# Centroid products moved behind the transposes, rounding steps and sums of x spread over the turns

## The chip, the cores and the metric

The kernel runs on one core of one Trainium2 chip. The metric is device microseconds of that core, the median of three runs: 996.82 us before the change (993.31 to 1000.97). The engines are called as the profile calls them: PE (matmul; PEld its weight loads), DVE (vector), ACT (scalar), POOL (GpSimd) and SP (here it only issues DMAs).

## The reference

Two blocks follow each other. The first is attention with a routing mask over 4 batches, 8 heads, 768 rows and 64 columns; each head has 16 centroids:

```
q_assign = argmax over c of  q_n . c_n      (q_n, k_n, c_n have length 1)
k_assign = argmax over c of  k_n . c_n
mask     = q_assign[:, None] == k_assign[None, :]
scores   = where(mask, q k^T / 8, -1e9)
attn     = softmax(scores);  x = attn v
```

A row thus attends to the rows that chose the same centroid. The second block takes x as 3072 rows of 512 columns:

```
h = x @ w_in            (512 to 2048)
g = h / (1 + exp(-1.702 h))
out = g @ w_out         (2048 to 512)
```

## The kernel before, in words

The kernel has two stages. The order of the instructions of every engine is the order in which the program issues them (a manual schedule), and each engine works through its own queue in that order.

**Attention.** Two heads of a batch are a pair; there are 16 pairs, 0 to 15. The loop over t (L636) has 96 turns and two more to drain. A turn takes two units. A unit is one block of 128 keys against half (384) of the queries, for both heads of the pair; six units, three turns, are a group, and two groups, six turns, are a pair. In what follows "turn 0" to "turn 5" are the six turns of a pair. In a turn the program issues, in this order:

- the scores of both units (L451), then the mask products (`part`, L466), which add a large negative number to the scores of pairs of rows with different centroids. They read rows of codes (`rows_of`) that DMAs have put in place;
- the exponentials on ACT (L474), and for the previous group the check of its row sums (`check`, L535 and L537, ACT);
- on POOL, the running sum of the exponentials over the six units of a group (`add_up`, L484, five additions of 128 x 768);
- the preparation of the next pair, if any is due in this turn (below);
- the value products of the two units of the turn before (L495), and after a group's last one a copy out of PSUM (L501);
- steps of the rounding of the weights (`step`, next paragraph);
- in turns 1 and 4, `normalise` of the group that ended: two row sums by matmul (L508), then on DVE a 32-block transposition (L511), a reciprocal (L513), a transposition back (L516) and a product (L522).

**Preparation of the next pair.** A list `PREP` has seven entries, and `prep_at` says in which of the six turns each is issued. Entries 0 and 1 are for q, 2 and 3 for k: one DVE transposition each of 128 x 768 (L305). Behind entry 1 and entry 3 the next load of q or k is issued (L134), ahead of entry 2 the load of v (L144), all on SP. Entry 4, `prep_near`, is the product of both with the centroids: eight small matmuls on PE (L326), sixteen records in the trace. Entry 5, `prep_assign`, is a chain on DVE from L349 to L389: the largest of the 16 products in each row, a code for the place where it stands, and its transposition. Entry 6, `prep_spread`, sends the codes through DRAM: four DMAs out (L396), then sixteen DMAs back (L403), which wait for the four. The mask products of the next pair need what these bring.

**Rounding.** The weights come in 64-bit form in 32 pieces. Each piece takes five DVE steps (L189, L193, L196, L200, L203), and `steps` says how many are issued in each of a pair's six turns. A piece begins with the issue of a later piece's load (L170), and its last step is followed by two instructions of ACT (L227, L230).

**PSUM and buffers.** `bank()` gives one of three PSUM banks in turn. Row sums, centroid products, assignment and rounding all take theirs there, so that the order of the calls says which bank a product has to wait for.

**Second block.** From L804 on, for each batch: matmuls of x with sums of w_in and of G with sums of w_out in seven products each (L716, L773), with the sums around them on DVE. For this the sums of x of a batch (`sums_x`, L598, with `differences`, L559) must stand: eight DVE instructions (L554). For the first batch they are issued in turn 76 of the attention; for the other batches between products of the batch before. The sums of the first weights (`sums_w`, L581) are four POOL instructions in each of the turns 72 and 78.

The functions that the change touches, and the loops that call them:

Of the kernel before, what the change touches and what calls it, by code (L numbers as in the profile page):

```python
# [38 lines left out]
def fast(  # L39
# [26 lines left out]
    nc = tc.nc  # L66
# [46 lines left out]
    def bank():  # L113
        return ps_m.tile([P, 512], FP32, name="m")

    def short():
        return tmp.tile([P, HALF], FP32, name="short")
# [154 lines left out]
    nc.vector.tensor_tensor(out=csq, in0=cent, in1=cent, op=ALU.mult)  # L272
    nc.vector.tensor_reduce(out=css, in_=csq, axis=AX.X, op=ALU.add)
    nc.gpsimd.tensor_tensor(out=cnorm, in0=css, in1=half, op=ALU.pow)
# [13 lines left out]
    for a in range(2):  # L288
# [4 lines left out]
                                         c=NC)[:, :, a, :])  # L293
# [3 lines left out]

    T, code, sT, hots = {}, {}, {}, {}

    def prep_turn(p, i):  # L300
        w, h = divmod(i, 2)
        if h == 0:
            T[p, w] = pairs.tile([P, S], FP32, name=f"T{w}")
            if p > 0:
# [41 lines left out]
    def prep_assign(p):  # L346
# [10 lines left out]
        best = asg.tile([P, n], FP32, name="best", bufs=1)  # L357
        nc.vector.tensor_reduce(out=best, in_=sc, axis=AX.X, op=ALU.max)
        eq = short().bitcast(BF16)[:, 0:n * NC].rearrange("p (n c) -> p n c",
# [8 lines left out]
        if p == 0:  # L368
            code[p] = asg.tile([P, n], FP32, name="code", bufs=1)
            nc.vector.tensor_reduce(out=code[p], in_=eq, axis=AX.X,  # L370
                                    op=ALU.max)
# [8 lines left out]
            in_=eq.rearrange("p (w j a) c -> p w j a c", a=2, j=NJ),  # L380
            axis=AX.X, op=ALU.max)
        nc.vector.scalar_tensor_tensor(
# [49 lines left out]
    PREP = [lambda p, i=i: prep_turn(p, i) for i in range(4)]  # L432
# [7 lines left out]
    s_of, A_of, sum_of, o_of, O_of, xT_of = {}, {}, {}, {}, {}, {}  # L440

    def split(g):
        return divmod(g, 2)
# [44 lines left out]
    def values(u):  # L488
        g, kt = divmod(u, NJ)
        p, h = split(g)  # L490
        if kt == 0:
            o_of[g] = ps_o.tile([P, 512], FP32, name="o")
        A = A_of.pop(u)
        for a in range(2):
            nc.tensor.matmul(out=o_of[g][a * D:(a + 1) * D, 0:HALF],  # L495
                             lhsT=v_in[p][:, a, kt, :], rhs=A[:, a, :],
                             start=(kt == 0), stop=(kt == NJ - 1))
        if kt == NJ - 1:
            O_of[g] = (xp if p < NPAIR - HP else xl).tile(
                [P, HALF], FP32, name="x")  # L500
            nc.scalar.copy(O_of[g], o_of.pop(g)[:, 0:HALF])  # L501

    def normalise(g):

        sm = sum_of.pop(g)
        ps = bank()
        for a in range(2):
            nc.tensor.matmul(out=ps[a * D:(a + 1) * D, 0:HALF], lhsT=twos,  # L508
                             rhs=sm[:, a, :], start=True, stop=True)
        turned = short()  # L510
        nc.vector.transpose(out=turned, in_=ps[:, 0:HALF])  # L511
        few = recs[g] = asg.tile([P, HALF // SQ], FP32, name="few")
        nc.vector.reciprocal(  # L513
            out=few, in_=turned.rearrange("p (n r) -> p n r", r=SQ)[:, :, 0])
        rec = short()
        nc.vector.transpose(  # L516
            out=rec.rearrange("p (n r) -> p n r", r=SQ),
            in_=few[:, :, None].broadcast_to((P, HALF // SQ, SQ)))
        p, h = split(g)
        b, hp = divmod(p, HP)  # L520
        x = O_of.pop(g)
        nc.vector.tensor_tensor(out=x, in0=x, in1=rec, op=ALU.mult)  # L522
        if b < B - 1:
            xT_of[b, h, hp] = x
        else:
            nc.sync.dma_start(out=kept[h, hp], in_=x)
# [25 lines left out]
    def sums(engine, todo):  # L552
        for o, a, op, b in todo:
            engine.tensor_tensor(out=o, in0=a, in1=b, op=(  # L554
                ALU.add if op == "+" else ALU.subtract))

    T_of = {}

    def differences(b):  # L559


        X = {(r, h, c): xT_of.pop((b, h, 2 * r + c))
             for r in range(2) for h in range(2) for c in range(2)}
        T = {(3, c): T_of[3, c] for c in range(2)}
        for c in range(2):
            T[1, c] = X[0, 1, c]
            sums(nc.vector, ((T[3, c], X[1, 1, c], "-", T[1, c]),
                             (T[1, c], T[1, c], "-", X[0, 0, c])))
        return X, T

    def A_in(row, col, f):

        at = (row * FB + f) * P
# [20 lines left out]

    def sums_x(b):  # L598

        X, T = differences(b)  # L600
        T.update(((i, c), T_of[i, c]) for i in (2, 4) for c in range(2))
        for c in range(2):
            sums(nc.vector, ((T[2, c], X[1, 1, c], "-", T[1, c]),))
        for c in range(2):
            sums(nc.vector, ((T[4, c], X[1, 0, c], "-", T[2, c]),))
        return X, T

    NT = NU // 2
    TG = NJ // 2

    prep_at = {}
    for p in range(1, NPAIR):
        for i in range(2 if p == 1 else 0, len(PREP)):
            t = 2 * TG * (p - 1) + (0, 0, 2, 2, 2, 3, 3)[i]
            prep_at.setdefault(t, []).append((p, i))
    loads = deque((p, w) for p in range(NPAIR) for w in range(2))
    for _ in range(3):  # L620
# [2 lines left out]
    def prep(p, i):  # L623
        if i == 2 and p:
            load_v(p)
        PREP[i](p)
        if i in (1, 3) and loads:
            load_qk(*loads.popleft())

    steps = (3, 1, 2, 0, 1, 4)  # L630
    XT = None
    for p, i in [(0, i) for i in range(6)] + [(1, i) for i in range(2)]:
        prep(p, i)
        if p == 0 and i in (1, 3):
# [1 line left out]
    for t in range(NT + 2):  # L636
        us = range(2 * t, 2 * t + 2) if t < NT else ()
        for u in us:
            scores(u)
        if t == 0:  # L640
            prep(0, 6)
        for u in us:
            part(u)
        for u in us:
            exps(u)
        if recs:
            check(*recs)
        for u in us:
            add_up(u)
        work = sorted(prep_at.get(t, ()), key=lambda w: PREP[w[1]] != prep_near)  # L650
        turns = [w for w in work if w[1] < 4]
        for p, i in turns:
            prep(p, i)
        work = [w for w in work if w[1] >= 4]
        while work and PREP[work[0][1]] == prep_near:
            prep(*work.pop(0))
        if 1 <= t <= NT:
            for u in range(2 * t - 2, 2 * t):
                values(u)
        if t in (NT - 24, NT - 18):  # L660
            sums_w(t // (NT - 18))
        if t == NT - 20:
            XT = sums_x(0)
        for p, i in work:
            prep(p, i)
        for _ in range(steps[t % (2 * TG)] if t > 2 else 0):
            step()
        if t >= 2 and (t - 2) % TG == TG - 1:
            normalise((t - 2) // TG)
# [134 lines left out]
    for b in range(B):  # L804
        for f in range(FB):
            first7(b, f, *XT)
            sums_w(b * FB + f + 2)
            if b == 0:
                sums_z(f)
        if b == 0:  # L810
            for h in range(2):
                for hp in range(HP):
                    x = xT_of[B - 1, h, hp] = xp.tile([P, HALF], FP32,
                                                      name="x")
                    nc.sync.dma_start(out=x, in_=kept[h, hp])
        for n in range(NH):
            sg = sums_g(n)
            if (b, n) == (B - 1, 0):


                ok = const.tile([P, 4, NW], FP32, name="ok")
                nc.vector.tensor_scalar(out=ok, in0=row_sums, scalar1=LIMIT,
                                        scalar2=None, op0=ALU.is_le)
                ok1 = const.tile([P, 1], FP32, name="ok1")
                nc.vector.tensor_reduce(out=ok1, in_=ok, axis=AX.XY, op=ALU.min)
            if (b, n) == (B - 1, 1):
                ps = bank()
                nc.tensor.transpose(out=ps[0:1, 0:P], in_=ok1, identity=ident)
                nc.vector.tensor_reduce(out=okt, in_=ps[0:1, 0:P], axis=AX.X,
                                        op=ALU.min)  # L830
                nc.vector.tensor_scalar(out=bad, in0=okt, scalar1=-1.0,
                                        scalar2=1.0, op0=ALU.mult, op1=ALU.add)
            if (b, n) == (B - 1, NH - 1):
                is_bad = nc.values_load(bad[0:1, 0:1], min_val=0, max_val=1)
            second7(b, n, sg)
            if n == 1 and b < B - 1:
                XT = sums_x(b + 1)
    return is_bad
@with_exitstack
def general(  # L840
# [436 lines left out]
```

## Time and profile before

| what | us |
|---|---|
| median of three runs | 996.82 |
| the profiled execution | 997.54 |
| its span, first to last instruction | 995.7 |
| start of pair 1's first turn | 38.90 |
| start of pair 15's first turn | 384.35 |
| first product of the second block | 409.30 |
| PE busy | 943.0 |
| DVE busy | 623.8 |
| POOL busy | 418.8 |
| ACT busy | 314.3 |

A line of a timeline is: start in us from the start of the span, time taken, engine, line of the kernel, operation, what is written and read, how many instructions are merged into the line, and in brackets the idle time before it and what ended it. A line of the waits is: who waited for whom, us in total, how often, the longest. In the slices of the span each digit is a fortieth of it, 24.9 us, in tenths of busy time; PEclk is the clock that PE was granted. Sums of busy time say little here, as PE is full in the second block and not in the first; so the turns are read one by one, from one first L451 to the next.

The turns of an ordinary pair are alike. In pair 9 they start at 231.95, 235.16, 239.01, 245.43, 248.63 and 252.48, and pair 10 starts at 255.69. Pairs 2 to 12 take 23.4 to 25.1 us each; pairs 13 and 14 take 31.7 and 25.6 us.

### The profile page before, as it was taken

Reading aid. Unit: us, or ns where it says so; the run is one execution under the profiler, and the core shown is the slowest. Engines: PE = TensorE matmul, PEld = TensorE weight load, DVE = VectorE, ACT = ScalarE, POOL = GpSimd, SP = SyncE. Lnnn points to the kernel's source line nnn. Section 1 sums busy time; section 2 is a strip of 40 time slices with the busy share of each in tenths; the row PEclk is TensorE's granted clock in tenths of the full one; section 3 lists DMA queues with packets and bytes.
Section 4 is the critical chain, followed back from the end, with each engine's and each line's share of the span. In section 5 each row is a group of like instructions: output and inputs, shape, how many; then the busy total and the mean of one; then the engine's idle time right before and its main releaser. Section 6 shows DMA issues by size and latency. Waiting matters only on the chain.

```text
span 995.7 us, 12731 instructions
## 1 busy us (share of the span) xinstructions
PE 943.0 (95%) x4565; PEld 569.6 (57%) x4565; DVE 623.8 (63%) x1029; ACT 314.3 (32%) x671; POOL 418.8 (42%) x308
## 2 busy tenths in 40 slices
PE   5998999999998789999999999999999999999997
PEld 3333333333333233455788655888655888556886
DVE  3678778877779985477634477534577434677431
ACT  3565565555655456322100122100222000222000
POOL 3878788777879678677400122000122000220000
PEclk8999999999999899999999999999999999999999
DMA  9344444544444311000200000000000000000000
GB/s 179 82 94 111 94 98 95 112 101 92 93 114 92 87 49 29 17 0 1 64 22 22 21 1 1 0 22 22 22 0 1 16 22 22 6 1 1 22 22 24
DMA packets 138440, 46.59 MB, mean 47 GB/s; under 512 B 127376, under 2 KB 132736, under 8 KB 138368
## 3 DMA queue, kind: packets, MB, share of 16 engines
q1 hardware_dynamic: 138224, 45.66, 20.2%
q8 instruction: 38, 0.62, 0.3%
q14 instruction: 34, 0.28, 0.1%
q10 hardware_dynamic: 144, 0.03, 0.0%
HBM read 37.63 MB, written 8.05 MB: 46 GB/s over the span
## 4 chain that ended last, share of the span: by engine, by line
PE 82%; DVE 12%; issue 3%; SPq 1%; DMA 1%; ACT 1%; POOL 0%; DVEq 0%; POOLq 0%; ACTq 0%
PE b L716 29%; PE b L773 29%; PE o L495 10%; PE s L451 9%; DVE T L305 2%; PE s L466 2%; PE m L508 2%; DVE short L516 1%; DVE short L511 1%; DVE e L200 1%; DVE x L522 1%; PE m L326 1%; DVE T L554 1%; DVE e L196 1%; DVE m L189 1%
## 5 line engine op out<-in xcount | busy, mean ns | idle before, releaser
L484 POOL TENSOR_TENSOR sum<-sum,A 128x768 f32<-128x768 f32 x128 | 243.3, 1901 | 32.0 <-ACT A L474 23.5
L474 ACT ACTIVATE A<-s 128x768 f32<-128x768 f32 x192 | 144.9, 806 | 158.6 <-PE s L466 157.0
L554 POOL TENSOR_TENSOR W<-w_in 128x256 f32<-128x256 f32 x32 | 23.8, 742 | 381.3 <-PE b L716 381.2
L707 DVE TENSOR_TENSOR G<-b,G 128x384 f32<-128x384 f32 x224 | 124.4, 556 | 64.6 <-PE b L716 51.4
L451 PE MATMUL s<-T,T 64*128 64x384 f32 x768 | 153.1, 518 | 4.4 <-ACT A L474 4.4
L495 PE MATMUL o<-A,inv 128*64 128x384 f32 x768 | 150.4, 515 | 0.0
L707 DVE TENSOR_TENSOR y<-b,y 128x256 f32<-128x256 f32 x72 | 29.4, 423 | 171.1 <-PE b L773 121.9
L544 ACT ACTIVATE th<-G 128x384 f32<-128x384 f32 x128 | 67.0, 523 | 210.1 <-DVE G L707 129.4
L451 PEld LDWEIGHTS s<-T,T 64*128 64x128 f32 x768 | 67.0, 189 | 89.6 <-ACT A L474 55.8
L545 DVE SCALAR_TENSOR_TENSOR G<-th,G 128x384 f32<-128x384 f32 x128 | 91.5, 715 | 22.8 <-ACT th L544 19.1
L716 PE MATMUL b<-x,W 128*128 128x384 f32 x256 | 93.0, 486 | 0.0
L716 PE MATMUL b<-T,w_in 128*128 128x384 f32 x256 | 93.0, 486 | 0.0
L716 PE MATMUL b<-x,w_in 128*128 128x384 f32 x256 | 89.9, 492 | 0.0
L773 PE MATMUL b<-Z,G 128*128 128x256 f32 x384 | 86.8, 379 | 0.0
L484 POOL TENSOR_TENSOR sum<-A 128x768 f32<-128x768 f32 x32 | 59.6, 1862 | 61.4 <-ACT A L474 61.3
L773 PE MATMUL b<-w_out,G 128*128 128x256 f32 x384 | 84.8, 379 | 0.0
L495 PEld LDWEIGHTS o<-A,inv 128*64 128x64 f32 x768 | 48.0, 140 | 57.0 <-issue 55.8
L773 PEld LDWEIGHTS b<-w_out,G 128*128 128x128 f32 x384 | 72.8, 190 | 10.9
L773 PEld LDWEIGHTS b<-Z,G 128*128 128x128 f32 x384 | 73.0, 190 | 9.9
L716 PEld LDWEIGHTS b<-x,w_in 128*128 128x128 f32 x256 | 49.1, 192 | 34.0 <-issue 1.2
L716 PEld LDWEIGHTS b<-x,W 128*128 128x128 f32 x256 | 48.6, 190 | 33.9
L716 PEld LDWEIGHTS b<-T,w_in 128*128 128x128 f32 x256 | 48.6, 190 | 33.9
(112 smaller groups left out, 1053.3 us busy)
## 6 DMA issues: line engine op xcount, KB each, us to landing
raw<-in_moe_w_in_dram SPq DMA_DIRECT2D x16, 512.0 KB
raw<-in_moe_w_out_dram SPq DMA_DIRECT2D x16, 512.0 KB
inv<-in_v_dram SPq DMA_DIRECT2D x16, 384.0 KB
in<-in_q_dram SPq DMA_DIRECT2D x60, 96.0 KB
in<-in_k_dram SPq DMA_DIRECT2D x60, 96.0 KB
rows<-line SPq DMA_DIRECT2D x240, 1.5 KB
out_dram<-y SPq DMA_DIRECT2D x12, 256.0 KB
out_dram<-y SPq DMA_DIRECT2D x24, 128.0 KB
```

The source lines that it names most:

```text
L305: nc.vector.transpose(out=T[p, w], in_=qk_in[p, w].rearrange("p j a d -> p (j a d)"))
L451: nc.tensor.matmul(out=ps[:, a, 0:HALF], lhsT=T[p, 1][rows, kt * P:(kt + 1) * P], rhs=T[p, 0][rows, h * HALF:(h + 1) * HALF], start=True, ...
L466: nc.tensor.matmul(out=s_of[u][:, a, :], lhsT=k_rows[r:r + n, kt * P:(kt + 1) * P], rhs=q_rows[r:r + n, h * HALF:(h + 1) * HALF], start=Fa ...
L474: nc.scalar.activation(out=A_of[u], in_=s_of.pop(u), func=AF.Exp, scale=SCALE)
L484: nc.gpsimd.tensor_tensor(out=sum_of[g], in0=A_of[u - 1] if kt == 1 else sum_of[g], in1=A_of[u], op=ALU.add)
L495: nc.tensor.matmul(out=o_of[g][a * D:(a + 1) * D, 0:HALF], lhsT=v_in[p][:, a, kt, :], rhs=A[:, a, :], start=(kt == 0), stop=(kt == NJ - 1))
L544: nc.scalar.activation(out=t, in_=h, func=AF.Tanh, scale=1.702)
L545: nc.vector.scalar_tensor_tensor(out=g, in0=t, scalar=1.0, in1=h, op0=ALU.add, op1=ALU.mult)
L554: engine.tensor_tensor(out=o, in0=a, in1=b, op=(ALU.add if op == "+" else ALU.subtract))
L707: nc.vector.tensor_tensor(out=o, in0=p, in1=a, op=ALU.add)
L716: nc.tensor.matmul(out=ps[:, 0:HALF], lhsT=a[:, c], rhs=x(c), start=(c == 0), stop=(c == 1))
L773: nc.tensor.matmul(out=ps[:, 0:DN], lhsT=a(f // 4)[:, f % 4], rhs=z(f), start=(f == 0), stop=(f == FB - 1))
```

## The change

Four things change in the attention stage.

1. k's transposition (entries 2 and 3, with their loads) goes from turn 2 to turn 1. The centroid products stay in turn 2, but are issued behind the value products of that turn instead of ahead of them.
2. The row sums (L508) become a function of their own, which is issued right behind the value products; the DVE part of `normalise` stays at the end of the turn.
3. The rounding steps of the six turns go from 3, 1, 2, 0, 1, 4 to 2, 0, 4, 0, 1, 4.
4. `sums_x` becomes a generator that issues one instruction for each `next`. For the first batch the eight are issued one in each of the turns 88 to 95 instead of all in turn 76. For the other batches all eight are still issued at one place, in a slightly different order.

```diff
-    def normalise(g):
+    def row_sums_of(g):
         sm = sum_of.pop(g)
-        ps = bank()
+        ps = ps_of[g] = bank()
         for a in range(2):
             nc.tensor.matmul(out=ps[a * D:(a + 1) * D, 0:HALF], lhsT=twos,
                              rhs=sm[:, a, :], start=True, stop=True)
+    ps_of = {}
+    def normalise(g):
+        ps = ps_of.pop(g)
...
     def sums_x(b):
-        X, T = differences(b)
-        T.update(((i, c), T_of[i, c]) for i in (2, 4) for c in range(2))
+        X = {(r, h, c): xT_of.pop((b, h, 2 * r + c))
+             for r in range(2) for h in range(2) for c in range(2)}
+        T = {(i, c): T_of[i, c] for i in (2, 3, 4) for c in range(2)}
         for c in range(2):
-            sums(nc.vector, ((T[2, c], X[1, 1, c], "-", T[1, c]),))
-        for c in range(2):
-            sums(nc.vector, ((T[4, c], X[1, 0, c], "-", T[2, c]),))
-        return X, T
+            T[1, c] = X[0, 1, c]
+        for o, a, z in ((3, (1, 1), 1), (1, 1, (0, 0)), (2, (1, 1), 1),
+                        (4, (1, 0), 2)):
+            for c in range(2):
+                one, two = (X[(*n, c)] if isinstance(n, tuple) else T[n, c]
+                            for n in (a, z))
+                sums(nc.vector, ((T[o, c], one, "-", two),))
+                yield X, T
...
-            t = 2 * TG * (p - 1) + (0, 0, 2, 2, 2, 3, 3)[i]
+            t = 2 * TG * (p - 1) + (0, 0, 1, 1, 2, 3, 3)[i]
...
-    steps = (3, 1, 2, 0, 1, 4)
-    XT = None
+    steps = (2, 0, 4, 0, 1, 4)
+    made = sums_x(0)
...
         work = [w for w in work if w[1] >= 4]
-        while work and PREP[work[0][1]] == prep_near:
-            prep(*work.pop(0))
         if 1 <= t <= NT:
             for u in range(2 * t - 2, 2 * t):
                 values(u)
+        if t >= 2 and (t - 2) % TG == TG - 1:
+            row_sums_of((t - 2) // TG)
+        while work and PREP[work[0][1]] == prep_near:
+            prep(*work.pop(0))
         if t in (NT - 24, NT - 18):
             sums_w(t // (NT - 18))
-        if t == NT - 20:
-            XT = sums_x(0)
+        if t >= NT - 8 and t < NT:
+            XT = next(made)
...
             if n == 1 and b < B - 1:
-                XT = sums_x(b + 1)
+                *_, XT = sums_x(b + 1)
```

More of the change, by code (lines that the diff above doesn't have):

```diff
@@ L557, in fast @@
     T_of = {}
[L559 to L564, printed above, removed]
-        for c in range(2):
-            T[1, c] = X[0, 1, c]
-            sums(nc.vector, ((T[3, c], X[1, 1, c], "-", T[1, c]),
-                             (T[1, c], T[1, c], "-", X[0, 0, c])))
-        return X, T
     def A_in(row, col, f):
@@ L598, in sums_x @@
     def sums_x(b):
-        X, T = differences(b)
-        T.update(((i, c), T_of[i, c]) for i in (2, 4) for c in range(2))
+        X = {(r, h, c): xT_of.pop((b, h, 2 * r + c))
+             for r in range(2) for h in range(2) for c in range(2)}
+        T = {(i, c): T_of[i, c] for i in (2, 3, 4) for c in range(2)}
         for c in range(2):
-            sums(nc.vector, ((T[2, c], X[1, 1, c], "-", T[1, c]),))
-        for c in range(2):
-            sums(nc.vector, ((T[4, c], X[1, 0, c], "-", T[2, c]),))
-        return X, T
+            T[1, c] = X[0, 1, c]
[6 more added lines that the diff above has]
+                yield X, T
     NT = NU // 2
```

## The prediction

> **What bounds the kernel now.** First the slices of the span, then the waits, then the order of time inside one pair.
>
> ```profile
> PE   5998999999998789999999999999999999999997
> ...
> POOL 3878788777879678677400122000122000220000
> PEclk8999999999999899999999999999999999999999
> ```
>
> After slice 16 (409 us) only the second block runs, with PE full; its code is almost untouched, and I leave its 586.4 us (409.3 to 995.7) alone. All the room is in the first 409 us, where POOL is almost as full as PE and the clock row has its dips. There the two waits of PE that matter here are:
>
> ```profile
> PE m L326 <- DVE T L305: 28.6, 14, 2.8
> ...
> PE s L466 <- DMA rows<-line: 2.7, 4, 0.9
> ```
>
> PE waits 28.6 us, in 14 pairs, for the second 32-block transposition (L305) before a centroid product (L326), and hardly at all (2.7 us) for the rows that DMAs bring to the mask products (L466). The order of time shows both in one pair, turn 2 of which starts at 239.01:
>
> ```profile
> 239.01 1.56 PE L451 MATMUL s<-T,T 64*128 64x384 f32 x8
> ...
> 243.52 0.53 PE L326 MATMUL m<-T,cT 128*32 128x192 f32 x8 [2.22 <-DVE T L305]
> ...
> 245.43 1.56 PE L451 MATMUL s<-T,T 64*128 64x384 f32 x8
> ...
> 246.53 0.36 DVE L364 TENSOR_TENSOR short<-short,rank 128x384 bf16<-128x384 bf16 x1
> ...
> 248.01 0.19 DVE L389 CAST row<-turned 128x64 bf16<-128x64 f32 x1
> ...
> 248.95 1.81 POOL L484 TENSOR_TENSOR sum<-A 128x768 f32<-128x768 f32 x1 [2.48 <-ACT A L474]
> ...
> 250.80 4.66 SPq L403 DMA_DIRECT2D rows<-line  x16
> ...
> 251.52 3.72 POOL L484 TENSOR_TENSOR sum<-sum,A 128x768 f32<-128x768 f32 x2 [0.76 <-ACT A L474]
> ...
> 252.48 1.56 PE L451 MATMUL s<-T,T 64*128 64x384 f32 x8
> ...
> 252.60 0.58 DVE L511 STREAM_TRANSPOSE short<-m 128x384 f32<-128x384 f32 x1 [3.80 <-PE m L508]
> ...
> 255.69 1.56 PE L451 MATMUL s<-T,T 64*128 64x384 f32 x8
> ...
> 257.75 2.19 DVE L200 SCALAR_TENSOR_TENSOR e<-raw,e 128x512 f32<-128x512 uint32 x1
> ...
> 259.86 0.96 DVE L305 STREAM_TRANSPOSE T<-in 128x768 f32<-128x768 f32 x1
> ```
>
> A turn starts with its first L451. A plain turn is 3.20 us (252.48 to 255.69), one with row sums 3.85 us, and turn 2 takes 6.42 us, 2.2 us of it PE idle before L326. Below, t is time after the start of turn 2. The rest of the pair is spaced so: the assignment runs on DVE from L349 (t = 5.72) to the end of L389 (t = 9.19), 3.47 us in all; then L396 and the sixteen L403 carry the rows to the next pair, whose first mask product stands 1.5 us into its turn 0, at t = 18.2.
>
> Two more stretches show what a late or crowded assignment costs:
>
> ```profile
> 317.86 1.75 DVE L364 TENSOR_TENSOR short<-short,rank 128x384 bf16<-128x384 bf16 x1
> ...
> 320.23 0.18 DVE L382 SCALAR_TENSOR_TENSOR codes<-codes 128x24 f32<-128x24 f32 x1
> 320.30 1.81 POOL L484 TENSOR_TENSOR sum<-A 128x768 f32<-128x768 f32 x1 [0.91 <-ACT A L474]
> ...
> 320.73 1.43 DVE L389 CAST row<-turned 128x64 bf16<-128x64 f32 x1
> ```
>
> ```profile
> 352.44 1.43 DVE L389 CAST row<-turned 128x64 bf16<-128x64 f32 x1
> ...
> 358.75 1.56 PE L451 MATMUL s<-T,T 64*128 64x384 f32 x8
> ...
> 362.48 0.32 PE L466 MATMUL s<-rows,rows 3*128 3x384 bf16 x1 [0.85 <-DMA rows<-line]
> ```
>
> L364, L382 and L389 take 0.36, 0.18 and 0.19 us in most pairs, but L364 and L389 took 1.75 and 1.43 us where a POOL sum (L484) was already running, and ended just when it did; L382 began 0.07 us before the sum and was not held up. In the third stretch L389 ended at 353.87, and the last mask product of the next pair, ready at about 360.28, ran at 362.48, when its row landed: 8.6 us after L389. That turn took 5.42 us. Other pairs issue the first L403 0.2 us sooner after L389 (2.60 against 2.84 us), so I take 8.4 us.
>
> **The change part by part.** Durations are of the profiled execution: 997.54 us, with 1.84 us outside its span of 995.7. The median shown is 996.82, 0.7 us lower.
>
> *Products behind the transposes.* k's transposition moves from turn 2 to turn 1, ahead of that turn's normalisation on DVE, and the sixteen matmul records of L326 move behind the value products of turn 2. On DVE the chain from the normalisation of turn 4 (L511 at 0.12 us after turn 5 starts), through 4 steps, q's transposition, 2 steps and k's, is done about 9.7 us after turn 5 starts, and the product is due 13.5 us after it (10.27 to turn 2, 3.21 of its work): the wait goes. Turn 2 is then 3.21 us and two groups of 0.46 us (243.52 to the value products at 243.98), 4.13 us; pair 0, whose transpositions are early, already has a turn 2 of 4.15 us. A pair without waits is 3 x 3.21 + 2 x 3.85 + 4.13 = 21.46 us. Pairs 1 to 14 took 345.45 us (38.90 to 384.35), so 14 such pairs (300.4 us) would save 45 us. On SP the loads of v and of the next q are issued a turn sooner, ahead of nothing urgent; both are used a pair later.
>
> *Rounding steps 3,1,2,0,1,4 become 2,0,4,0,1,4.* Still 11 a pair. But turn 2's four steps stand on DVE between the normalisation and the assignment. Turn 5 of before has just this order, L511 and then four steps, and what follows there starts 5.73, 6.02, 6.61, 7.34 or 7.38 us after the turn's start (7.38 above: 252.48 to 259.86), by which of the five kinds of step come; the kinds turn by one each pair. So L349 starts at t = 5.7 to 7.4, no earlier than before, while everything after turn 2 is 2.3 us earlier. L364 starts 1.80 us behind L349 (244.73 to 246.53), at t = 7.5 to 9.2.
>
> *What that meets on POOL.* In turns 3 and 4 the sums start 3.52 and 6.09 us after turn 3 starts (248.95 and 251.52 against 245.43), which with the shorter turn 2 is t = 7.65 and 10.22; they end at 9.46 and 12.03, and a third fills 12.1 to 13.9. Before, turn 3 started at t = 6.42 and the first sum at 9.94, so the assignment lay in POOL's pause. In four of five pairs L364 now starts inside the first sum and ends at 9.46 + 0.21 = 9.67 (0.21 as at 319.40 to 319.61); L382 follows at 10.29 (0.62 later, as at 319.61 to 320.23), 0.07 us after the second sum has begun: it waits for 12.03 and ends at 12.07, and L389, at 12.39, meets the third and ends at t = 13.97. In the fifth pair (steps ending in L196) L364 is through at 7.89, L382 waits for 9.6 and L389 is done at 10.1.
>
> *What is late next.* The last mask product of the next pair's turn 0 could run at t = 4.13 + 3.21 + 3.85 + 3.21 + 1.52 = 15.92 and must wait for L389 + 8.4. Four pairs of five: 13.97 + 8.4 - 15.92 = 6.45 us; the fifth 2.6 us. PE's queue is in order, so value products and the next scores wait behind it. DVE has what it needs to recover: it is free by about t = 25, and the next normalisation is not due before t = 28.
>
> *The clock.* In the slice 50.77 to 54.18 the granted clock was 0.50, after a stretch of 3.41 us in which PE sat idle 1.83 us; that cost such turns 1.4 to 1.6 us (7.82 against about 6.3). A pause of 6.45 us always leaves such a stretch, 1.5 us; one of 2.6 us about 0.9. By the Trainium skill, TensorE: Matmul & The Clock Gate, section on HAM oscillation, only idle gaps above about 3.4 us matter, which the 1.83 us here contradicts; by that rule the short pauses would be free and the sum 3 us lower.
>
> *First batch's sums of x.* Eight DVE instructions (L554) leave turn 76, where they stretched from 322.08 to 332.5 and held ACT 7.2 us behind L516, and go one a turn to turns 88 to 95. That gain is inside the 345.45 us already (pairs 13 and 14 took 31.7 and 25.6 us). In the last groups each holds POOL 0.55 us, and PE waits for POOL's last sum (2.2 us before the end): I take 1.3 us, between 0 and 4. The row sums' own move changes nothing on PE, where no instruction comes between. Their bank is one that the assignment freed a turn or more before; if it were not, PE would wait for DVE, at most the 2.2 us of today.
>
> *Sum.* Of pairs 1 to 14, eleven wait 6.45 us (71.0), two 2.6 and one, with POOL's weight sums in its turn 0, about 4.1 (9.3); clock 11 x 1.5 + 3 x 0.9 = 19.2. 300.4 + 71.0 + 9.3 + 19.2 - 345.45 = +54.5. Pair 1's first rows, now assigned after the later product: +1. Weight sums elsewhere +0.5, sums of x +1.3. In all +57, **1055 us**.
>
> The one close race is L382 against the second sum. The rows next to it are a step L200 that began 0.11 us after a POOL instruction and waited it out (308.49, 1.18 us long), and an L364 that began 0.05 us before one and did not (28.74). I take the wait, as 0.07 is nearer to the 0.11 on the same side. The Trainium skill, SBUF — State Buffer, section "SBUF: two separate sides", states that whichever of the two starts first has the shared port pair for the whole instruction and the other fully blocks; by it the sum is 1055, and by a race won 1034.
>
> **The rivals.** *L382 wins the race.* L389 then waits only for the second sum and ends at t = 12.1: 4.6 us in eleven pairs, 20 us less: 1034 us. *The old wait is exchanged for one as long.* If the assignment met no sum, L389 would end 3.47 us after those five starts, at 9.2 to 10.9, mean 10.1; waits of 10.1 + 8.4 - 15.92 = 2.6 us, 36 us, with 6 us of clock: 300.4 + 42 - 345.45 + 2.8 = 0, about 997 us. The 1.75 and 1.43 above speak against it. *The transfer is hidden and the 45 us come.* If rows were there in time, 997.5 - 45 + 2.8 = 955 us. That needs L389 done by t = 7.5, before L349 would even have started in most pairs, or rows 5 us faster. It decides from a mean wait and clock cost under 3.0 us a pair (42 us / 14); below that the kernel gets faster. For it speaks that before shows only 2.7 us of waits for rows.
>
> **How the numbers follow.** Forecast 0.50; race won, or one wait less than I count, 0.21; exchange 0.15; hidden 0.14. Within 1% (987 to 1007 us) is about what a measurement of this kernel can tell from no change: most of the exchange, 0.11. Faster: hidden, 0.14. Slower: the rest, 0.75. The forecast's own range is 1040 to 1068 (clock and wait of the eleven pairs by 1 us each way). The whole range leaves out the hidden case and an overshoot: 990 to 1070.
>
> **What would show it.** In the profile after: no wait of L326 for L305; turn 2 at 4.1 us; L364 and L389 long in most pairs; a wait of PE L466 for DMA rows of 50 to 90 us in sum; turn 0 of pairs 2 to 15 at 9 to 11 us; more dips of the clock. Wrong if L364 and L389 stay short, or if turn 0 stays near 3.2 us.

## The result, and the profile after

| what | before, us | after, us |
|---|---|---|
| median | 996.96 (4 runs) | 1078.62 (4 runs) |
| profiled execution | 997.54 | 1077.39 |
| its span | 995.7 | 1075.6 |
| first product of the second block | 409.23 | 489.88 |
| start of pair 1, of pair 15 | 38.90, 384.35 | 39.18, 455.26 |

The changed kernel is slower: a ratio of 1.082, 95% interval 1.078 to 1.087. All 80 us are lost before the second block starts, which takes what it took (586.5 us before, 585.7 after). Its first matmul starts at 409.23 us in the kernel before, not at 409.30 as given further up.

Lines behind the change have moved in the code: the normalisation's L511, L516 and L522 are L517, L522 and L528 after, L554 is L560; lines up to L501 are as before. The slices of the span first, as the page of the changed kernel has them:

```profile
PE   6977779888878889979999999999999999999997
...
POOL 3855766555556676765771002200022200021000
PEclk8988888888888888989999999999999999999999
```

The first 18 slices are the attention now. PE, which had 9 in most of them, has mostly 7 and 8; POOL, which was almost as full as PE, has mostly 5 to 7; and the clock row, nearly all 9 before, has 8 in most slices. In the waits of the changed kernel the wait of L326 for L305 is gone, and another has taken its place:

```profile
PE s L466 <- DMA rows<-line: 74.4, 42, 3.4
```

It was 2.7 us in sum. The order of time shows where it comes from. This is the assignment for pair 7, with turn 2 at 200.68 and the next pair's turn 0 at 214.93:

```profile
200.68 1.56 PE L451 MATMUL s<-T,T 64*128 64x384 f32 x8
...
204.67 1.56 PE L451 MATMUL s<-T,T 64*128 64x384 f32 x8
...
208.19 1.81 POOL L484 TENSOR_TENSOR sum<-A 128x768 f32<-128x768 f32 x1 [0.44 <-ACT A L474]
...
209.11 1.10 DVE L364 TENSOR_TENSOR short<-short,rank 128x384 bf16<-128x384 bf16 x1
...
210.76 7.55 POOL L484 TENSOR_TENSOR sum<-sum,A 128x768 f32<-128x768 f32 x4 [0.76 <-ACT A L474]
210.84 1.77 DVE L382 SCALAR_TENSOR_TENSOR codes<-codes 128x24 f32<-128x24 f32 x1
...
212.92 1.59 DVE L389 CAST row<-turned 128x64 bf16<-128x64 f32 x1
...
214.93 1.56 PE L451 MATMUL s<-T,T 64*128 64x384 f32 x8
...
217.20 4.64 SPq L403 DMA_DIRECT2D rows<-line  x16
...
219.46 0.50 PE L466 MATMUL s<-rows,rows 3*128 3x384 bf16 x1 [2.97 <-DMA rows<-line]
...
221.70 0.57 PE L466 MATMUL s<-rows,rows 3*128 3x384 bf16 x2 [1.74 <-DMA rows<-line]
...
222.93 0.47 PE L466 MATMUL s<-rows,rows 3*128 3x384 bf16 x1 [0.66 <-DMA rows<-line]
```

L364 starts at 209.11 inside the first sum of POOL (208.19 to 210.00) and ends 0.21 us after it. L382 starts 0.08 us after the second sum began and takes 1.77 us instead of 0.18; L389 starts inside the third and takes 1.59 instead of 0.19. The waits thus show as longer instructions, not as idle time. L389 ends 13.84 us after turn 2 started. The sixteen DMAs follow, and the last mask product, which could run at 216.45, runs at 222.93. This repeats: in thirteen of the fourteen pairs 1 to 14 L389 ends at 13.84 us, to 0.01 us, and in thirteen pairs (2 to 13 and 15, the long pairs below) turn 0 takes 11.1 to 11.7 us.

The same stretch in the granted clock (each line is a stretch of the span: its length, busy time and instructions of PE, PEld, DVE, ACT and POOL, then the clock, the DMA share and GB/s):

```profile
215.24:218.65 3.41, 1.25 (x8) 0.39 (x4) 3.24 (x5) 2.07 (x8) 2.99 (x2) 1.00 0.04 5
218.65:228.89 10.24, 7.02 (x20) 2.32 (x20) 5.70 (x9) 2.19 (x4) 1.81 (x1) 0.50 0.57 120
228.89:232.30 3.41, 3.41 (x24) 1.56 (x24) 0.81 (x2) 1.51 (x2) 1.87 (x2) 1.00 1.03 148
```

The clock is half for 10.24 us, although PE works again from 222.93 on: turn 0 takes 11.17 us and turn 1, which waits for nothing, 5.22 instead of 3.85.

### The profile page after: what moved, and what is told of

The parts are those of the page before. It is cut to its first block, busy times and chain, and to the rows that moved or that the text cites. A ratio compares the mean times of both kernels' runs of the same rounds, so it can differ in the third digit from the quotient of the medians.

```text
span 1075.6 us, 12735 instructions
## 1 busy us (share of the span) xinstructions
PE 983.0 (91%) x4565; PEld 583.1 (54%) x4565; DVE 669.4 (62%) x1029; ACT 320.6 (30%) x671; POOL 413.5 (38%) x308
## 4 chain that ended last, share of the span: by engine, by line
PE 69%; DVE 18%; SPq 7%; DMA 4%; issue 2%; POOL 1%; ACT 0%; DVEq 0%; POOLq 0%; ACTq 0%
PE b L768 27%; PE b L711 27%; PE o L495 7%; SPq L403 5%; PE s L451 5%; DVE codes L382 2%; DVE row L389 2%; DVE x L528 2%; DVE e L200 2%; DMA rows<-line 2%; DMA line<-row 2%; PE s L466 1%; SPq L396 1%; DVE short L364 1%; PE m L508 1%
## 5 line engine op out<-in xcount | busy, mean ns | idle before, releaser
L484 POOL TENSOR_TENSOR sum<-sum,A 128x768 f32<-128x768 f32 x128 | 239.8, 1873 | 75.1 <-ACT A L474 65.9
L560 POOL TENSOR_TENSOR W<-w_in 128x256 f32<-128x256 f32 x32 | 23.4, 732 | 381.3 <-PE b L711 381.2
L451 PE MATMUL s<-T,T 64*128 64x384 f32 x768 | 166.8, 557 | 0.7 <-ACT A L474 0.7
L495 PE MATMUL o<-A,inv 128*64 128x384 f32 x768 | 164.5, 555 | 0.0
L451 PEld LDWEIGHTS s<-T,T 64*128 64x128 f32 x768 | 72.8, 205 | 91.2 <-ACT A L474 39.7
L466 PE MATMUL s<-rows,rows 3*128 3x384 bf16 x360 | 47.7, 354 | 74.6 <-DMA rows<-line 74.4
L466 PEld LDWEIGHTS <-rows 3*128 3x128 bf16 x360 | 13.3, 92 | 139.9 <-DMA rows<-line 92.5
L517 DVE STREAM_TRANSPOSE short<-m 128x384 f32<-128x384 f32 x32 | 18.5, 578 | 110.0 <-PE m L508 110.0
L495 PEld LDWEIGHTS o<-A,inv 128*64 128x64 f32 x768 | 50.9, 148 | 61.4 <-issue 60.7
```

The lines of the kernel that those rows point to most:

```text
L451: nc.tensor.matmul(out=ps[:, a, 0:HALF], lhsT=T[p, 1][rows, kt * P:(kt + 1) * P], rhs=T[p, 0][rows, h * HALF:(h + 1) * HALF], start=True, ...
L466: nc.tensor.matmul(out=s_of[u][:, a, :], lhsT=k_rows[r:r + n, kt * P:(kt + 1) * P], rhs=q_rows[r:r + n, h * HALF:(h + 1) * HALF], start=Fa ...
L484: nc.gpsimd.tensor_tensor(out=sum_of[g], in0=A_of[u - 1] if kt == 1 else sum_of[g], in1=A_of[u], op=ALU.add)
L495: nc.tensor.matmul(out=o_of[g][a * D:(a + 1) * D, 0:HALF], lhsT=v_in[p][:, a, kt, :], rhs=A[:, a, :], start=(kt == 0), stop=(kt == NJ - 1))
L560: engine.tensor_tensor(out=o, in0=a, in1=b, op=(ALU.add if op == "+" else ALU.subtract))
```

## The experiments

Theory A: the four steps ahead of the assignment push three of its instructions, L364, L382 and L389, into POOL's sums; each of them waits until the sum that began ahead of it has ended; the rows are late, PE waits, and its clock is halved. Theory B: the four steps cost their own time and no more, and POOL is no matter. Times are medians; each ratio is to runs of the kernel before on the same chip, with its 95% interval.

**e1: the steps alone.** The kernel before, with one line changed:

```diff
-    steps = (3, 1, 2, 0, 1, 4)
+    steps = (2, 0, 4, 0, 1, 4)
```

> The kernel before, with only the rounding steps of the six turns changed to 2, 0, 4, 0, 1, 4. Theory A (the steps push the assignment into POOL's sums, whose instructions it waits out one after the other, so that the rows come late): behind k's transposition and four steps L349 starts 6.7 to 8.3 us after turn 2, the sums stand at 9.7, 12.3 and 14.2, and L389 ends at 11.6 to 16.0; the next pair's mask products wait 2.0 to 6.4 us, and the old wait for the transposition stays: about 1065 us, 1045 to 1080. Theory B (the steps only take their own time, POOL is no matter): L389 ends at 10.1 to 11.8, waits of 0.5 to 2.2 us, about 1015 us.

Measured: 1040.84 us, ratio 1.044 (1.038 to 1.051). Above B's 1015, and below A's range by 4 us. L389 ended at 11.4 to 11.9 us in most pairs and at 12.96 and 15.84 in two, where I expected 11.6 to 16.0. The steps alone do half of the harm. The size was off because all three instructions waited in only one of the fourteen pairs. In six pairs L382 began 0.46 to 0.62 us inside a sum, and L389 came in the pause behind it; in seven L382 came ahead of a sum and it was L389 that waited one out, as here in the assignment for pair 7:

```profile
194.57 0.18 DVE L382 SCALAR_TENSOR_TENSOR codes<-codes 128x24 f32<-128x24 f32 x1
194.68 1.81 POOL L484 TENSOR_TENSOR sum<-A 128x768 f32<-128x768 f32 x1 [2.45 <-ACT A L474]
...
195.07 1.47 DVE L389 CAST row<-turned 128x64 bf16<-128x64 f32 x1
```

L382 begins 0.11 us before the sum and takes its 0.18 us; L389 begins 0.39 us after it and waits it out. A tenth of a microsecond decides about a sum's length.

**e2: the products' place with the old steps.** The kernel after, with the line of e1 turned back.

> The kernel after, with the rounding steps of before (3, 1, 2, 0, 1, 4). Theory A: L349 starts 4.6 to 6.1 us after turn 2, and in four pairs of five L389 ends at 9.9, in the fifth at 13.7; waits for rows of 2.5 and 6.3 us: about 1020 us, 1005 to 1035. A rival, that the products' new place and not the steps does the harm: as slow as the changed kernel, 1070 to 1080 us.

Measured: 1016.70 us, ratio 1.020 (1.014 to 1.026). L389 ended at 9.87 us (to 0.01) in ten pairs, at 13.84 in two and at 10.5 in two, much as theory A has it. So what is left of the change without the steps costs some 20 us: the old wait of 28.6 us is saved, and the shorter pair leaves the rows too little time. The move of the row sums and of the sums of x is in this run too; the row sums' move was not run by itself.

**e3: the sums of x alone.** The kernel before, with `sums_x` as a generator and its eight instructions in turns 88 to 95.

> The kernel before, with only the first batch's sums of x issued one a turn in turns 88 to 95. Theory: pairs 12 to 14 (24.3, 31.7 and 25.6 us) go to about 23.8 each, 10 us less, and the end of the attention gives about 1.3 us back: 988 us, 984 to 992. The rival, that eight instructions that each wait out a sum of POOL cost as much late as early: 997 us.

Measured: 992.54 us (10 runs), ratio 0.995 (0.992 to 0.998). A small gain, 5 to 6 us where 10 were expected. Pairs 12, 13 and 14 took 27.0, 27.2 and 25.3 us: pair 13 lost its 31.7, but in pairs 12 and 13 turns 2 and 3 still took 8.6 and 4.3 to 4.5 us. POOL's four weight sums stand in turn 0 of just these two pairs. The trace fits them as the start of it: a POOL sum that begins right behind them ends 3.7 us after turn 2 starts instead of 2.8 to 3.2, the product L522 waits it out, and with it k's transposition, so that L326 waits 2.75 us instead of 1.9 to 2.2; the clock is then half for 6.83 us. A run without the weight sums there was not made.

**e4: the steps behind the assignment.** The kernel after, with

```diff
-    steps = (2, 0, 4, 0, 1, 4)
+    steps = (2, 0, 0, 4, 1, 4)
```

> The kernel after, with turn 2's four rounding steps issued in turn 3, behind the assignment (2, 0, 0, 4, 1, 4). Theory A: L349 starts 4.1 us after turn 2, when the product is there; L364 waits for the last sum of the group (end at 6.75), L382 comes at 7.6, just after the next group's first sum began at 7.5, and waits until 9.3; L389 ends at 9.9 in every pair: waits of 2.5 us, about 1000 us, 990 to 1015. Theory B (POOL is no matter): L389 ends at 7.6, no wait worth naming, about 960 us.

Measured: 1002.90 us (10 runs, 996.6 to 1012.5), ratio 1.006 (1.002 to 1.009). L349 started at 4.13 us and L389 ended at 9.86 to 10.08 in every pair, as theory A says to 0.2 us; B's 960 is out. Moving four steps by one place is worth 76 us against the changed kernel.

**e5: the assignment in PSUM.** The kernel after; only `prep_assign` is changed: `sc` and `ps` lie in the PSUM bank of the products, and the comparison, its rank and the turned codes stay there, so that no arithmetic instruction of it reads two SBUF operands and the last copy does not go from SBUF to SBUF:

```diff
+        if p > 0:
+            nc.vector.tensor_tensor(
+                out=sc, in0=sc, in1=best[:, :, None].broadcast_to((P, n, NC)),
+                op=ALU.is_equal)
+            nc.vector.tensor_tensor(
+                out=sc, in0=sc, in1=rank[:, None, :].broadcast_to((P, n, NC)),
+                op=ALU.mult)
+            first = ps[:, n * NC:n * NC + n]
...
+            nc.vector.tensor_copy(out=codes[:, 0, 0:n], in_=first)
+            nc.vector.scalar_tensor_tensor(
+                out=codes[:, 1, 0:n], in0=first, scalar=0.5 / CODE,
+                in1=codes[:, 0, 0:n], op0=ALU.mult, op1=ALU.mult)
+            turned = ps[:, 512 - 2 * SQ:512]
...
```

> The kernel after, with the assignment's intermediate results kept in its PSUM bank, so that no DVE instruction of it has two SBUF inputs or copies from SBUF to SBUF (one copy of 24 columns more); order and steps as after. Theory A: none of its instructions waits for a sum of POOL, L389 ends 3.9 us behind L349's start, 9.6 to 11.3 us after turn 2, instead of 13.84; waits of 2.3 to 3.9 us: about 1013 us, 1000 to 1030. Theory B (the lateness is the time of the four steps itself): within 5 us of 1078.

Measured: 1018.44 us, ratio 1.024 (1.016 to 1.032), 60 us less than the changed kernel with the same order of work. The last copy (L389 of the kernel after, L379 here) ended 3.97 us behind L349's start in nearly every pair, whatever POOL did. In the assignment for pair 8 L363, L372 and L379, which do the work of L364, L382 and L389, all begin inside sums and take only 0.57, 0.18 and 0.22 us:

```profile
209.41 1.81 POOL L507 TENSOR_TENSOR sum<-A 128x768 f32<-128x768 f32 x1 [0.42 <-ACT A L497]
...
211.10 0.57 DVE L363 TENSOR_TENSOR m<-m,rank 128x384 f32<-128x384 f32 x1
...
211.97 3.71 POOL L507 TENSOR_TENSOR sum<-sum,A 128x768 f32<-128x768 f32 x2 [0.76 <-ACT A L497]
...
212.51 0.18 DVE L372 SCALAR_TENSOR_TENSOR codes<-m,codes 128x24 f32<-128x24 f32 x1
...
213.03 0.22 DVE L379 CAST row<-m 128x64 bf16<-128x64 f32 x1
```

**e6: both.** The assignment as in e5 and the steps as in e4.

> Both: the assignment in PSUM as in e5 and turn 2's four steps behind it as in e4. Theory A: L349 at 4.1 us after turn 2, L389 ends at 8.0, the rows land 0.6 us after the mask products could run; pairs of about 22 us, no half clock: 962 us, 955 to 975. If the DMAs' own time or the late normalisation becomes the bound: 980 us or more.

Measured: 973.14 us, ratio 0.977 (0.971 to 0.984): faster than either kernel. The last copy ended at 8.11 us in twelve of fourteen pairs (9.3 in the other two), turns 0 took 3.9 to 6.0 us from pair 2 on, and the half clock all but went (3.4 us in the attention from pair 1 on, against 122.9 us after). What is left of the wait (L489 is the mask product here):

```profile
PE s L489 <- DMA rows<-line: 10.5, 17, 1.0
```

**e7: PE kept busy.** The kernel after, in which the second unit's scores of turn 0 are computed eight times:

```diff
-        for a in range(2):
+        n = 7 if p > 1 and h == 0 and kt == 1 else 0
+        for a in [0, 1] * (n + 1):
...
+            n -= a
...
-                             start=True, stop=False)
+                             start=True, stop=n + a > 0)
```

> The kernel after, in which PE repeats the scores of the second unit of turn 0 seven times from pair 2 on (fourteen matmuls, 5.2 us, their results overwritten by the same values), in the time in which it waits for the rows. If half the clock costs what I read from the turns (turn 0 at 11.17 against 9.7, turn 1 at 5.2 against 3.85, 2.9 us a pair), PE stays at the full clock and 13 pairs gain it: about 1041 us, 1036 to 1050. If the clock is a bystander: 1078 us. If the repeats take longer than the wait: more than 1078 us.

Measured: 1056.53 us, ratio 1.062 (1.054 to 1.070): 22 us less by doing more. In nine of the thirteen long pairs the clock stayed whole, turn 0 took 9.5 to 10.1 us and turn 1 3.85; in the other four it still dropped late in turn 0, and these four gained only 1 us in all, which is why 22 us were gained and not 37. The stretch of turns 0 and 1 of pair 7, as above:

```profile
208.16:222.00 13.84, 12.30 (x75) 5.80 (x74) 9.26 (x13) 6.03 (x14) 6.09 (x4) 1.00 0.39 83
```

The clock is 1.00, where the same two turns of the changed kernel had half the clock for 10.24 us; they take 13.84 us together against 16.39. The 2.6 us between are the price of the clock alone, as the rows came no sooner: the last mask product ran 22.55 us after turn 2 here and 22.26 in the changed kernel.

**e8: eight row DMAs instead of sixteen, on e6.** One DMA now writes the two partitions that get the same codes:

```diff
-            for r in range(SQ * a, P, 2 * SQ):
-                for w, b, to in ((0, 0, 0), (0, 1, 1), (1, 0, 0), (1, 1, 2)):
...
-                        out=rows_of[w, p % 2][r + to:r + to + 1, :],
...
+            for w, b, to in ((0, 0, 0), (0, 1, 1), (1, 0, 0), (1, 1, 2)):
...
+                r = SQ * a + to
...
+                    out=rows_of[w, p % 2][r:r + 2 * SQ + 1:2 * SQ, :],
...
+                        "j t -> (j t)")[None, :].broadcast_to((2, S)))
```

> As e6, and the sixteen DMAs of L403 become eight, each of which writes the same codes to two partitions. At 0.29 us of issue each, the last rows should land about 2.3 us sooner, 6.1 us behind the end of L389 instead of 8.4. With L389 done 8.1 us after turn 2 the rows are then there at 14.2, before the mask products at 15.8: no wait, turn 0 at 3.2 us instead of 3.9 to 6.0 (mean 4.5): about 954 us, 948 to 963. If the rows' time is not in the issue: as e6, 973.

Measured: 962.76 us, ratio 0.968 (0.964 to 0.972), the fastest kernel here. The expected 954 was missed: turn 0 takes 3.4 to 5.0 us from pair 2 on. SP's queue shows why:

```profile
234.25 3.97 SPq L426 DMA_DIRECT2D rows<-line  x8
```

Eight take 3.97 us to issue where sixteen took 4.65: 0.50 us each instead of 0.29. Here the time to issue went with the number of partitions written more than with the number of DMAs; other sizes were not tried.

**e9: the same on the kernel after.**

> The kernel after, with eight row DMAs instead of sixteen and nothing else changed. If PE's wait in turn 0 is the end of the chain L389, L396, L403, it gets shorter by the 2.3 us that the issue loses, in 13 pairs, with the half clock as it is: about 1046 us, 1035 to 1055. If the wait has another cause, or the time lies in the transfers: 1078.

Measured: 1064.37 us, ratio 1.069 (1.065 to 1.073), 14 us less than after and 9 above the expected range. L389 still ended at 13.84, and the last mask product ran at 21.7 instead of 22.3 us after turn 2: the wait follows the DMAs, by the 0.6 us that they gained and not by 2.3. In thirteen pairs that makes 8 us; most of the rest goes with the clock, which was half for 6.83 us in each long pair, where nine of the thirteen had 10.24 us after.

**e10: no sums of POOL beside the assignment.** The kernel after, but the second group's sums are only those of its last two units; DVE's instructions are the same.

```diff
-        if kt == 0:
+        if kt == 0 or g % 2 and kt < NJ - 1:
             return
-        if kt == 1:
+        if kt == 1 or g % 2:
```

> The kernel after, leaving out four of the five POOL additions of every second group (that group's row sums are then those of its last two units alone), so that no sum of POOL runs while the assignment does; DVE's instructions are those of after. Theory A: L364, L382 and L389 take 0.36, 0.18 and 0.19 us, L389 ends 3.5 us behind L349's start, 9.2 to 10.9 us after turn 2, waits of 1.9 to 3.6 us: about 1010 us, 995 to 1025. Theory B (the lateness is the time of the four steps itself): within 5 us of 1078.

Measured: 1009.38 us, ratio 1.016 (1.010 to 1.022). B is out: with POOL's four additions gone the kernel is 69 us faster, though no DVE instruction was touched. The assignment for pair 8, whose L364 would have started inside a sum:

```profile
208.49 0.36 DVE L364 TENSOR_TENSOR short<-short,rank 128x384 bf16<-128x384 bf16 x1
...
209.47 0.18 DVE L382 SCALAR_TENSOR_TENSOR codes<-codes 128x24 f32<-128x24 f32 x1
...
209.97 0.20 DVE L389 CAST row<-turned 128x64 bf16<-128x64 f32 x1
```

All three take their short times, and L389 ends 3.49 us behind L349's start. What this kernel still loses against the kernel before is the later place itself: L349 starts no earlier in a shorter pair, and PE still waits 30.3 us for rows.

## Why the prediction was right in its mechanism and too low

It said slower, by 57 us, with 990 to 1070 us as the range; it is 82 us slower, and 1078.6 us lies above the range, which left out an overshoot. Two steps failed: the term for the clock, 1.5 us a long wait where 2.8 were lost, and, in one pair of five, L364 against POOL's first sum, which it took as won by 0.12 us and which was lost by 0.02. By its own steps:

- **The old wait goes.** Right: L326 waits for nothing. Turn 2 takes 3.99 us, where 4.13 was predicted.
- **The assignment starts no earlier.** Right: L349 starts at 5.67 to 7.37 us, the predicted 5.7 to 7.4.
- **What it meets on POOL.** Right in the chain of three waits: L389 ends at 13.84, predicted 13.97. The close race was lost by L382 in all thirteen pairs where it was run against the second sum, always by 0.07 to 0.09 us, as predicted. The Trainium skill, SBUF — State Buffer, section "SBUF: two separate sides", says that whichever of the two starts first keeps the port pair that DVE and GpSimd share, for its whole instruction. The runs agree down to 0.02 us: an L364 that began 0.02 us after a sum took 2.00 us, and one that began 0.03 us before one took 0.36.
- **The fifth pair.** Wrong in two of three. L364 was to start at 7.53, before the sum at 7.65, with 0.12 us to spare. The turn that was 0.14 us shorter put the sum at 7.51: in the assignments for pairs 4 and 9 L364 came 0.02 us late, and they waited like the others. In the third, for pair 14, L364 came 0.03 us early and it went as predicted. First pair 4, then pair 14:

```profile
116.17 1.80 POOL L484 TENSOR_TENSOR sum<-A 128x768 f32<-128x768 f32 x1 [0.77 <-ACT A L474]
116.19 2.00 DVE L364 TENSOR_TENSOR short<-short,rank 128x384 bf16<-128x384 bf16 x1
...
422.88 0.36 DVE L364 TENSOR_TENSOR short<-short,rank 128x384 bf16<-128x384 bf16 x1
...
422.92 2.00 POOL L484 TENSOR_TENSOR sum<-A 128x768 f32<-128x768 f32 x1 [0.82 <-ACT A L474]
```

  Predicted for the two were 2.6 us and 0.9 us of clock each; it was 6.5 and about 2.8. The two pairs cost 11.6 us more with their clock, 8.9 of it beyond what the point on the clock counts.
- **Rows 8.4 us behind L389.** Right: 22.26 - 13.84 = 8.42 us in most pairs; the wait of 6.45 us measured about 6.5.
- **The clock.** The mechanism was right, the size was half. The term was 1.5 us a long wait, from stalls of 2 us in the kernel before, after which one stretch of 3.41 us ran at half the clock. In the first of these two rows of the kernel before PE is busy for only 1.58 us; the second has the half clock:

```profile
47.36:50.77 3.41, 1.58 (x24) 0.61 (x24) 2.88 (x5) 2.82 (x9) 3.30 (x2) 1.00 0.64 158
50.77:54.18 3.41, 3.41 (x12) 1.24 (x10) 3.20 (x8) 0.78 (x2) 1.86 (x2) 0.50 0.97 167
```

  Behind a wait of 6.5 us there are two or three such stretches (10.24 us in nine of the thirteen long pairs, 6.83 in four), and the last is spent after PE is back. By turns 0 and 1, which took 16.36 us on average in the thirteen long pairs, 9.30 more than the 7.06 without waits, 6.5 is the wait and 2.8 the clock; e7's nine pairs at the whole clock gave 2.0 to 3.0 for the clock, 2.7 on average. Thirteen times 1.35 us is 17.6 us. The Trainium skill, TensorE: Matmul & The Clock Gate, section "What's actually happening", says that the clock comes back after a whole busy window of about 3.4 us that does not follow the program; the half clock until 228.89, when PE was back at 222.93, agrees with it, and I had not counted that window.
- **Sums of x.** Predicted as part of the pairs; the late ones cost 0.9 us at the end (25.76 us from pair 15's start without its wait, 24.88 before), 1.3 predicted.

Sum of the misses: clock +17.6, two pairs +8.9, shorter turn 2 -2.0, pair 14's wait -0.7: +23.8, against 1078.6 - 1055 = 23.6 us (22.6 us by the two profiled executions, 997.54 and 1077.39, from which the misses are read).

Of the rivals, "L382 wins the race" (1034) fell to every pair. "Exchange" (997) had as its condition an assignment that meets no sum; e10 makes it so and took 1009, as turns 0 and 1 lost 60 us in its fourteen pairs where the rival had 42. "Hidden" (955) comes near in e8 (963), which needed three changes more. That the steps before the assignment, the sharing with POOL and the DMAs are each a link is shown by e4, e5 and e10, and e9; that the weight sums are what remains in e3 is not shown by a run.

## What to carry to other kernels

A wait that is removed on the critical engine shortens the time that something else was hidden in; the next chain has to be timed to the tenth of a microsecond against the shortened turn before the order is changed, and instructions that cannot run beside a busy neighbour's have to be placed in its pauses. A queue position that costs nothing by instruction count can be worth 76 us where it also puts three short instructions into sums of 1.8 us. An idle stretch of PE is to be priced with the clock behind it, here some 2.8 us for one of 6.5 us, and not with the idle time alone.

## What the runs showed of the hardware that was not expected

A DMA that writes two partitions took 0.50 us to issue against 0.29 us for one, so that half as many saved 0.7 us of 4.65. Extra matmuls in a wait made the kernel 22 us faster, as they held the clock. And a race of 0.07 us was lost in all thirteen pairs, and in e7 and e9 again by 0.07 to 0.09 us: where L364 has waited for the first sum, L382 starts 0.83 us after that sum's end whenever L364 began, and the second sum 0.76 us after it.
